# Pooled attention and a three-way maxout: the order of the first batch's loads, its size found in two steps, and a new order of the first seven groups

## The chip, the cores and the metric

The program runs on one core of one Trainium2 chip. The metric is the device time of one execution in microseconds (us): 1984.18 before, the median of three runs (1984.15 to 1985.3). The core has five engines with instruction queues of their own: TensorE (PE in the profile) multiplies matrices, VectorE (DVE), ScalarE (ACT) and GpSimd (POOL) work elementwise, and SyncE (SP) issues the DMAs here. Each engine takes its instructions in the order in which they are written; between engines and DMAs semaphores say what has to be done first.

## The reference

```python
kv_pool = kv.reshape(B, H // r, r, W // r, r, C).mean(axis=(2, 4))   # B=4, H=384, W=32, r=4, C=128
k = v = kv_pool.reshape(B, -1, C) @ w_sr                             # 768 keys in each batch
s = (q @ k.transpose(0, 2, 1)) / np.sqrt(C)                          # q: 4 x 12288 x 128
a = np.exp(s - s.max(-1, keepdims=True))
a /= a.sum(-1, keepdims=True) + 1e-09
x = (a @ v).reshape(-1, C)                                           # 49152 x 128
h = np.maximum(np.maximum(x @ w1, x @ w2), x @ w3)                   # 768 hidden columns
out = h @ w_out
```

The four weights of the last two lines come as float64. The kernel takes them apart with integer operations on their two 32-bit words.

## The kernel before

The 49152 rows of q are cut into 96 groups of 512 rows, 24 for each batch, and a group into 4 tiles of 128 rows. Nearly every product is made in three float16 matmuls: each operand is split into a high part and the remainder (`_hi` and `_lo`, or `hh`/`hl`, `xh`/`xl`), and the product of the two remainders is left out. The split needs a power of two for a scale, so each operand's largest value is found first.

The program is one list of steps, written out as tokens in the strings of START, STEADY and END (lines 159 to 214). `run` (line 1026) reads them in order, and `step` (line 888) takes the next piece of work of that kind. START covers the loads, the weights and the first groups; STEADY, two groups long, is run 45 times; END finishes the last groups. The place of a token sets the place of its instructions on each engine. Their meaning:

- `S`: one tile's 128 x 768 scores on PE, 6 matmuls, into `ps_s`, which has two buffers. `m`: the row maximum `mx` and the bias `nb` on DVE. `e`: the exponential `a` on ACT, which frees `ps_s`. `c`: its float16 part on ACT, into `ahl`, which has three buffers. `l`: the remainder on POOL, and then the DMA that turns the tile into `aT`.
- `X`: half of a group's attention product on PE (18 matmuls of 512 columns); for group 0 a quarter, one tile at a time (`attend_tile`). `xh`, `xl`: its split on ACT and DVE.
- `H`: one of six hidden steps of a group, 6 matmuls into the two buffers of `ps_h`. `R`: the first of its two halves on ACT. `M`: the maximum `h` of both on DVE. `C`, `L`: its split, on ACT and POOL. `O`: the output product, 3 matmuls (6 with the last hidden step of a group). The third of the three hidden products is avoided: two are made with differences of the weights (`d_hi`, `d_lo`), and `w1` comes in through one product `w1o` of w1 and w_out.
- `P`, `G`, `T`: the output is turned by a DMA (`o_turned`), merged and scaled on DVE, and stored.
- `qd`, `qc`, `qp`, `qe`, `qh`, `ql`: load of q, its scaling by column on POOL, its size, and its split and turn.
- `kd`, `ka`: load and pooling of the next batch's kv. In START the first batch has tokens of its own: `kv.s.i` loads piece i of third s (512 KB each, 12 pieces), `add` and `fold` sum pieces on DVE (or POOL), `gat` and `end` sum 128 columns at a time on PE by matmuls with the identity, `gathered_peak` takes the third's maximum, `turn_tops` and `tops` the maximum over thirds and partitions (by one matmul and a reduction), `sized` the scale `k_up` from it, `gathered_project` multiplies by w_sr, and `gathered_hi`, `gathered_lo` write the keys `k_hi`, `k_lo`.
- `w` and a letter, with the weight and its half: `wd` loads, `wm` scales the upper words (ACT), `ws`, `wl`, `wn` put the words together on DVE (`w_e`), `wr` takes the difference from w1 (POOL), `wt` the maximum, `dsize`, `dsized` the scale, `wh`, `wo` the split.

A `!` behind a token puts it on DVE, a `%` on POOL (for `qp!`, the sum on ACT). The kv pieces and the weight halves share the 13 buffers of `kvp`, which are given out in turn, so the fourteenth load waits until the first one's readers are done, and so on. SP's queue is in order too: a load that waits for its buffer holds up all that is issued behind it, turns (DMA_TRANSPOSE) included. At the end, `last_hidden` and `last_max` (lines 734 and 748) do the last hidden step in two halves, and `last_project` and `last_finish` the last output.

Of the kernel before, what the change touches and what calls it, by code (L numbers as in the profile page):

```python
# [20 lines left out]
def kernel(  # L21
# [338 lines left out]

    def turn_w1(h):
# [705 lines left out]
```

## Time and profile before

| | us |
|---|---|
| median of three runs | 1984.18 |
| the profiled execution | 1984.26 |
| its span, first to last instruction | 1982.5 |
| PE busy in the span | 1957.7 |
| ACT busy | 1491.2 |
| DVE busy | 1451.0 |
| POOL busy | 1314.9 |

The granted TensorE clock is 1.00 over the span. PE is the engine to watch: what it is idle, or what its work grows by, is the time that a change can move. All instructions carry one line, L104, that of the helper which keeps the written order, so the rows are read by the names of tiles: output, arrow, inputs, then partitions x elements and type, and the count. Times in the rows are us from the span's start.

### The profile page before, as it was taken

Reading aid. Unit: us, or ns where it says so; the run is one execution under the profiler, and the core shown is the slowest. Engines: PE = TensorE matmul, PEld = TensorE weight load, DVE = VectorE, ACT = ScalarE, POOL = GpSimd, SP = SyncE. Lnnn points to the kernel's source line nnn. Section 1 sums busy time; section 2 is a strip of 40 time slices with the busy share of each in tenths; the row PEclk is TensorE's granted clock in tenths of the full one; section 3 lists DMA queues with packets and bytes.
Section 4 is the critical chain, followed back from the end, with each engine's and each line's share of the span. In section 5 each row is a group of like instructions: output and inputs, shape, how many; then the busy total and the mean of one; then the engine's idle time right before and its main releaser. Section 6 shows DMA issues by size and latency. Waiting matters only on the chain.

```text
span 1982.5 us, 29471 instructions
## 1 busy us (share of the span) xinstructions
PE 1957.7 (99%) x9813; PEld 959.1 (48%) x9813; DVE 1451.0 (73%) x2531; ACT 1491.2 (75%) x2617; POOL 1314.9 (66%) x959
## 2 busy tenths in 40 slices
PE   5999999999999999999999999999999999999999
PEld 5544444444444444444444444444444444444444
DVE  8777777777766777777767777777767666767677
ACT  4777777777777777777777777777777777777774
POOL 3577766766666666766766666766676666666653
PEclk9999999999999999999999999999999999999999
DMA  8677776676678777766668667866677666756663
GB/s 276 122 150 161 169 153 137 129 143 135 127 154 163 156 154 152 141 139 136 132 126 168 153 147 165 162 125 133 136 137 142 126 125 125 150 121 126 132 128 81
DMA packets 844761, 284.50 MB, mean 144 GB/s; under 512 B 818240, under 2 KB 819392, under 8 KB 844608
## 3 DMA queue, kind: packets, MB, share of 16 engines
q1 hardware_dynamic: 844608, 282.61, 69.6%
q8 instruction: 77, 1.26, 0.3%
q14 instruction: 76, 0.62, 0.1%
HBM read 53.54 MB, written 25.17 MB: 40 GB/s over the span
## 4 chain that ended last, share of the span: by engine, by line
PE 96%; DMA 2%; DVE 1%; ACT 0%; POOL 0%; issue 0%; SPq 0%; DVEq 0%; ACTq 0%
PE ps_h L104 37%; PE ps_o L104 22%; PE ps_x L104 19%; PE ps_s L104 18%; DMA aT<-ahl 1%; DMA kv_piece<-in_kv_dram 1%; DMA kv_piece<-in_moe_w_dram 0%; POOL ahl L104 0%; DMA o_turned<-o_planes 0%; DVE kv_piece L104 0%; DVE w_e L104 0%; SPq L104 0%; ACT a L104 0%; DVE mx L104 0%; DVE o_sb L104 0%
## 5 line engine op out<-in xcount | busy, mean ns | idle before, releaser
L104 POOL TENSOR_TENSOR hl<-h,hh 128x512 f16<-128x512 f32 x473 | 566.3, 1203 | 488.4 <-ACT hh L104 487.4
L104 POOL TENSOR_TENSOR ahl<-a,ahl 128x768 f16<-128x768 f32 x382 | 635.3, 1682 | 119.6 <-ACT ahl L104 79.8
L104 DVE SCALAR_TENSOR_TENSOR h<-ps_h,h 128x512 f32<-128x512 f32 x575 | 396.7, 690 | 372.9 <-PE ps_h L104 214.3
L104 ACT ACTIVATE h<-ps_h 128x512 f32<-128x512 f32 x575 | 342.6, 596 | 282.6 <-PE ps_h L104 272.4
L104 PE MATMUL ps_h<-xh,d_hi 128*128 128x512 f16 x1150 | 435.8, 379 | 0.3 <-DVE h L104 0.2
L104 PE MATMUL ps_h<-xl,d_hi 128*128 128x512 f16 x1150 | 435.8, 379 | 0.0
L104 PE MATMUL ps_h<-xh,d_lo 128*128 128x512 f16 x1150 | 435.8, 379 | 0.0
L104 DVE TENSOR_REDUCE mx<-ps_s 128x1 f32<-128x768 f32 x384 | 365.5, 952 | 55.2 <-PE ps_s L104 55.0
L104 ACT ACTIVATE a<-ps_s,nb,q_sc 128x768 f32<-128x768 f32 x384 | 379.1, 987 | 6.3 <-DVE nb L104 5.1
L104 PE MATMUL ps_s<-k_hi,qT 128*128 128x384 f16 x1536 | 374.8, 326 | 4.9 <-ACT a L104 4.5
L104 PE MATMUL ps_x<-aT,v_hi 128*128 128x512 f16 (+1 forms) x1188 | 366.6, 373 | 0.7 <-DMA aT<-ahl 0.6
L104 ACT CAST hh<-h 128x512 f16<-128x512 f32 x577 | 335.3, 613 | 42.0 <-DVE h L104 41.4
L104 PEld LDWEIGHTS <-d_hi 128*128 128x128 f16 x2308 | 225.7, 98 | 256.5 <-issue 0.3
L104 PE MATMUL ps_o<-hh,wo 128*128 128x512 f16 x1140 | 339.0, 379 | 0.0
L104 PEld LDWEIGHTS <-qT 128*128 128x128 f16 x2304 | 225.3, 98 | 194.0 <-issue 6.8
L104 ACT CAST ahl<-a 128x768 f16<-128x768 f32 x375 | 306.4, 829 | 7.7 <-DMA aT<-ahl 1.9
L104 PEld LDWEIGHTS <-wo 128*128 128x128 f16 x1710 | 167.3, 98 | 191.8 <-DVE wo L104 0.2
L104 PE MATMUL ps_s<-k_lo,qT 128*128 128x384 f16 x768 | 250.4, 326 | 0.3 <-DVE k_lo L104 0.3
L104 PE MATMUL ps_x<-aT,v_lo 128*128 128x512 f16 (+1 forms) x594 | 220.2, 373 | 0.0
L104 PE MATMUL ps_o<-hl,wo 128*128 128x512 f16 x570 | 216.0, 379 | 0.0
L104 PEld LDWEIGHTS <-v_hi 128*128 128x128 f16 x1188 | 115.4, 98 | 135.0 <-DMA aT<-ahl 0.8
L104 PEld LDWEIGHTS <-d_lo 128*128 128x128 f16 x1154 | 112.9, 98 | 122.1 <-issue 2.5
(142 smaller groups left out, 1420.2 us busy)
## 6 DMA issues: line engine op xcount, KB each, us to landing
q_sb<-in_q_dram SPq DMA_DIRECT2D x48, 512.0 KB, 4.3
kv_piece<-in_kv_dram SPq DMA_DIRECT2D x48, 512.0 KB, 4.3
out_dram<-o_sb SPq DMA_DIRECT2D x95, 256.0 KB, 2.0
aT<-ahl SPq DMA_TRANSPOSE x384, 4.0
kv_piece<-in_moe_w_dram SPq DMA_DIRECT2D x6, 384.0 KB, 6.2
qT<-q_hl SPq DMA_TRANSPOSE x96, 3.6
o_turned<-o_planes SPq DMA_TRANSPOSE x95, 3.4
kv_piece<-in_moe_w_out_dram SPq DMA_DIRECT2D x2, 384.0 KB, 5.0
```

Of the source, the lines that this page charges most:

```text
L104: return lambda **kw: tc.keep_in_program_order(op(**kw))
```

## The change

It has five parts.

1. A new START. It covers seven groups where the old one covered one, and STEADY is run 42 times instead of 45; both give the same steps in all, and the steps done when the first common STEADY begins are the same. In its first strings q, one weight half (`wd.0.0`) and all twelve kv pieces are loaded, and the other weight halves behind them. The three `fold` steps are gone, and five `add`s (one of them on POOL, `add.0.0.1%`) stand where three stood, so that the gathers on PE go from 62 to 56.
2. The first batch's size is found in two steps. `early_tops` takes the maximum of thirds 0 and 2, over partitions too; `last_tops` brings that of third 1 alone; `first_sized` takes the larger one and makes the scale with integer operations (the exponent's bits and their complement) in place of a reciprocal; `first_exps` makes what hangs on it, later. The scale is another power of two than before, and g_exp and o_down follow it.
3. Tokens are taken apart: `lt`, `qt`, `Pt` and `Tt` issue the turns and the store that stood inside `l`, `ql`, `P` and `T`; `qu` is the second half of `qp`; `turned_w1` and `produced` the second halves of `turn_w1` and `product`. STEADY and END have the new tokens right behind the old ones.
4. The first tile's scores have the four matmuls with `k_hi` ahead of the two with `k_lo`; `gathered_project` for third 2 takes a buffer of `ps_s` instead of `ps_o`.
5. In END `last_max` stands ahead of the last but one group's `G` and `T`.

The core of the diff (of START, whose effect the rows further down show, only its first strings):

```diff
-    W_SIGNS = 3
+    W_SIGNS = 2
...
-        "sr qd qc! qc! srh wd.1.1 wm.1.1 wd.2.0 wm.2.0! ws.2.0 wd.0.0 ws.1.1 wl.2.0 wn.2.0 kv.2.1",
+        "qd wd.0.0 kv.2.2 kv.2.0 sr kv.2.1 kv.0.0 gat.2.2.4 kv.2.3 kv.0.1 wm.0.0! kv.0.3 qc! kv.0.2 qc! srh",
+        "kv.1.1 add.2.0.1 qp! kv.1.0 kv.1.2 gat.2.0.4 end.2.3.4 qu add.0.0.1% qh kv.1.3 ws.0.0 ql add.0.2.3",
...
-        "L! G T O last_hidden O O last_max last_project.3 last_project.4 last_project.5 last_finish",
+        "C L! L! O last_hidden O O last_max G T Tt last_project.3 last_project.4 last_project.5 last_finish",
...
-                self.kps[1] = ps_o.tile([P, NJ, C], F32, name="ps_o").rearrange("p j c -> p (j c)")
+                self.kps[1] = two_banks()[:, 0]
...
+        def early_tops(self, s, n):
+            dve.tensor_reduce(out=self.m[:, KS:KS + 1], in_=self.m[:, s:n + 1:n - s], axis=AX.X, op=ALU.max)
+            self.tops_ps = spare(True)
+            mm(out=self.tops_ps[:, :P], lhsT=self.m[:, KS:KS + 1].to_broadcast([P, P]), rhs=ident, start=True, stop=True)
+        def early(self):
+            self.least = tiny.tile([P, 1], F32, name="least", bufs=1)
+            dve.tensor_reduce(out=self.least, in_=self.tops_ps[:, :P], axis=AX.X, op=ALU.max)
+            dve.tensor_scalar(out=self.least, in0=self.least, scalar1=TINY, scalar2=None, op0=ALU.max)
+        def first_sized(self):
+            dve.tensor_scalar(
+                out=self.g, in0=self.g, scalar1=self.least, scalar2=2.0 ** -12, op0=ALU.max, op1=ALU.mult
+            )
+            dve.tensor_scalar(
+                out=self.up.bitcast(I32), in0=self.g.bitcast(I32), scalar1=EXPO, scalar2=EXPO,
+                op0=ALU.bitwise_and, op1=ALU.bitwise_xor,
+            )
...
+        terms = [(h, i) for h in range(2) for i in range(3)]
+        if (g, j) == (0, 0):
+            terms.sort(key=lambda t: t[1] == 2)
...
-    for _ in range(NG // 2 - 3):
+    for _ in range(NG // 2 - 6):
         run(STEADY)
```

On SP, at the start of the program, the loads stand as follows in before (-) and now (+). `in_moe_w_dram` are w1, w2 and w3, `in_kv_dram` the kv pieces.

```order
 L104 DMA wsr_sb<-in_w_sr_dram 128x128
 L104 DMA q_sb<-in_q_dram 128x1024
+L104 DMA kv_piece<-in_moe_w_dram 128x768
+L104 DMA kv_piece<-in_kv_dram 128x1x1024 x12
 L104 DMA kv_piece<-in_moe_w_dram 128x768 x3
-L104 DMA kv_piece<-in_kv_dram 128x1x1024
+L104 DMA q_sb<-in_q_dram 128x1024
 L104 DMA kv_piece<-in_moe_w_dram 128x768
-L104 DMA kv_piece<-in_kv_dram 128x1x1024 x4
+L104 DMA_TRANSPOSE qT<-q_hl 128x8x128
 L104 DMA kv_piece<-in_moe_w_dram 128x768
```

All twelve kv pieces have moved ahead of five of the six halves of w1, w2 and w3 and of the second load of q.

On DVE, from the first batch's keys on, these rows stood in before:

```order
L104 SCALAR_TENSOR_TENSOR k_lo<-ps_x,k_up,k_hi 128x512
L104 SCALAR_TENSOR_TENSOR k_lo<-ps_o,k_up,k_hi 128x256
L104 TENSOR_SCALAR w_e<-w_e 128x384
L104 TENSOR_REDUCE mx<-ps_s 128x1
L104 TENSOR_SCALAR nb<-mx,q_sc 128x1
L104 TENSOR_REDUCE mx<-ps_s 128x1
L104 TENSOR_SCALAR nb<-mx,q_sc 128x1
L104 TENSOR_SCALAR w_e<-w_e 128x384
L104 SCALAR_TENSOR_TENSOR w_e<-kv_piece,w_e 128x384 x3
```

And in the changed kernel, at the same place:

```order
L104 SCALAR_TENSOR_TENSOR k_lo<-ps_x,k_up,k_hi 128x512
L104 SCALAR_TENSOR_TENSOR k_lo<-ps_s,k_up,k_hi 128x256
L104 TENSOR_SCALAR w_e<-w_e 128x384
L104 SCALAR_TENSOR_TENSOR w_e<-kv_piece,w_e 128x384
L104 TENSOR_SCALAR q_sc<-q_row,g_exp 128x1
L104 TENSOR_REDUCE mx<-ps_s 128x1
L104 TENSOR_SCALAR nb<-mx,q_sc 128x1
L104 SCALAR_TENSOR_TENSOR w_e<-kv_piece,w_e 128x384
L104 TENSOR_REDUCE mx<-ps_s 128x1
L104 TENSOR_SCALAR nb<-mx,q_sc 128x1
L104 SCALAR_TENSOR_TENSOR w_e<-kv_piece,w_e 128x384
```

The weight passes (`w_e`) that before were mostly done by then stand between the row maxima now.

On DVE, at the end of the program, behind the last remainders of full width (`o_turned` is the last but one group's output, the 256 wide rows are the last hidden step's halves):

```order
-L104 COPY o_sb<-o_turned 128x2x512
-L104 TENSOR_SCALAR rs<-sm,o_down 128x4
-L104 RECIPROCAL rs<-rs 128x4
-L104 SCALAR_TENSOR_TENSOR o_sb<-o_sb,w_down,rs 128x512
-L104 SCALAR_TENSOR_TENSOR h<-ps_s,h_23182 128x256
-L104 SCALAR_TENSOR_TENSOR h<-ps_s,h_23186 128x256
+L104 SCALAR_TENSOR_TENSOR h<-ps_s,h_23172 128x256
+L104 SCALAR_TENSOR_TENSOR h<-ps_s,h_23176 128x256
 L104 TENSOR_TENSOR hl<-h,hh 128x256 x2
+L104 COPY o_sb<-o_turned 128x2x512
+L104 TENSOR_SCALAR rs<-sm,o_down 128x4
+L104 RECIPROCAL rs<-rs 128x4
```

The last hidden step's maxima and remainders have moved ahead of the merge and the scaling of the group before.

More of the change, by code (lines that the diff above doesn't have):

```diff
@@ L359, in sized_u, with keep_warm @@
         times(w1o_up, d_up[0], u_up[0], H_DOWN)
+    def keep_warm(n):
+        if "warm" not in st:
+            st["warm"] = ps_o.tile([P, G], F32, name="ps_o")
+        w = ident.bitcast(F16)
+        for _ in range(n):
+            mm(out=st["warm"][:, :2 * P], lhsT=w[:, :P], rhs=w, start=True, stop=True)
     def turn_w1(h):
@@ L365, in turn_w1, with turned_w1 @@
             tr(out=ps[:, t * P:(t + 1) * P], in_=W[0, h].values()[:, t * P:(t + 1) * P], identity=ident)
-        act.copy(out=w1T[h], in_=ps[:, :HALF_F])
+        W["turned", h] = ps
+    def turned_w1(h):
+        act.copy(out=w1T[h], in_=W.pop(("turned", h))[:, :HALF_F])
     def product_w1():
@@ L376, in product_w1, with produced_w1 @@
             )
+        W["product"] = ps
+    def produced_w1():
+        ps = W.pop("product")
         act.mul(out=w1o[:, 0], in_=ps[:, :C], mul=w1o_up)
@@ L452, in gathered_project, with gathered_hi @@
             )
-        def gathered_hi(self, n):
+        def gathered_hi(self, n, on=None):
             ps, ks = (self.kps[n], slice(0, G)) if n == 0 else (self.kps[n][:, :PW], slice(G, NK))
-            act.mul(out=self.k_hi[:, ks], in_=ps, mul=self.up)
+            if on:
+                on.tensor_scalar(out=self.k_hi[:, ks], in0=ps, scalar1=self.up, scalar2=None, op0=ALU.mult)
+            else:
+                act.mul(out=self.k_hi[:, ks], in_=ps, mul=self.up)
         def gathered_lo(self, n):
@@ L490, in peak, with turn_tops @@
             )
-        def turn_tops(self, first=False):
+        def turn_tops(self):
             dve.tensor_reduce(out=self.m[:, KS:KS + 1], in_=self.m[:, :KS], axis=AX.X, op=ALU.max)
-            self.tops_ps = spare(first)
+            self.tops_ps = spare(False)
             mm(
@@ L498, in turn_tops, with last_tops, first_exps @@
             )
+        def early_tops(self, s, n):
+            dve.tensor_reduce(out=self.m[:, KS:KS + 1], in_=self.m[:, s:n + 1:n - s], axis=AX.X, op=ALU.max)
+            self.tops_ps = spare(True)
+            mm(
+                out=self.tops_ps[:, :P], lhsT=self.m[:, KS:KS + 1].to_broadcast([P, P]), rhs=ident,
+                start=True, stop=True,
+            )
[3 more added lines that the diff above has]
+            dve.tensor_scalar(out=self.least, in0=self.least, scalar1=TINY, scalar2=None, op0=ALU.max)
+        def last_tops(self, s):
+            self.tops_ps = spare(True)
+            mm(
+                out=self.tops_ps[:, :P], lhsT=self.m[:, s:s + 1].to_broadcast([P, P]), rhs=ident,
+                start=True, stop=True,
+            )
+        def first_sized(self):
+            dve.tensor_scalar(
+                out=self.g, in0=self.g, scalar1=self.least, scalar2=2.0 ** -12, op0=ALU.max, op1=ALU.mult
+            )
+            dve.tensor_scalar(
+                out=self.up.bitcast(I32), in0=self.g.bitcast(I32), scalar1=EXPO, scalar2=EXPO,
+                op0=ALU.bitwise_and, op1=ALU.bitwise_xor,
+            )
+        def first_exps(self):
+            dve.tensor_scalar(
+                out=self.g.bitcast(I32), in0=self.g.bitcast(I32), scalar1=EXPO, scalar2=None, op0=ALU.bitwise_and
+            )
+            times(self.g_exp, self.g, SCALE * 2.0 ** -19)
+            times(self.o_down[:, 0:1], self.up, O_DOWN / A_UP)
+            times(self.o_down[:, 1:2], self.up, O_DOWN * 1e-9)
         def tops(self):
@@ L537 @@
     KT = {}
-    st = {x: {} for x in ("q", "qr", "ps", "qT", "sc", "sm", "nb", "aT", "x", "hp", "h", "a", "turned", "split", "qhl", "xh", "h1")}
+    st = {x: {} for x in ("q", "qr", "ps", "qT", "sc", "sm", "nb", "aT", "x", "hp", "h", "a", "turned", "split", "qhl", "xh", "h1", "ahl")}
     def q_load(s):
@@ L562, in q_peak, with q_up @@
             dve.tensor_reduce(out=row, in_=st["q"][s], axis=AX.XY, op=ALU.max, apply_absolute_value=True)
+        st["qr"][s] = row
+    def q_up(s):
+        row = st["qr"][s]
         up = qp.tile([P, 1], F32, name="q_up", bufs=2)
@@ L610, in scores @@
         st["ps"][g, j] = two_banks()[:, :, :HALF]
-        for h in range(2):
-            for i, (s_, kk) in enumerate(((0, k.k_hi), (1, k.k_hi), (0, k.k_lo))):
-                mm(
-                    out=st["ps"][g, j][:, h], lhsT=qT[:, j, s_], rhs=kk[:, h * HALF:(h + 1) * HALF],
-                    start=i == 0, stop=i == 2,
-                )
+        terms = [(h, i) for h in range(2) for i in range(3)]
+        if (g, j) == (0, 0):
+            terms.sort(key=lambda t: t[1] == 2)
+        for h, i in terms:
+            s_, kk = ((0, k.k_hi), (1, k.k_hi), (0, k.k_lo))[i]
+            mm(
+                out=st["ps"][g, j][:, h], lhsT=qT[:, j, s_], rhs=kk[:, h * HALF:(h + 1) * HALF],
+                start=i == 0, stop=i == 2,
+            )
     def soft_bias(g, j, negated):
@@ L645, in soft_lo, with soft_turn @@
         a, ahl = st["a"].pop((g, j))
+        (on or pool).tensor_tensor(out=ahl[:, 1], in0=a, in1=ahl[:, 0], op=ALU.subtract)
+        st["ahl"][g, j] = ahl
+    def soft_turn(g, j):
         if g not in st["aT"]:
             st["aT"][g] = ap_.tile([P, 2 * NKT, G], F16, name="aT")
-        (on or pool).tensor_tensor(out=ahl[:, 1], in0=a, in1=ahl[:, 0], op=ALU.subtract)
+        sp_dma.dma_start_transpose(
+            out=st["aT"][g][:, :, j * P:(j + 1) * P], in_=st["ahl"].pop((g, j)).rearrange("p s k -> p (s k)")
+        )
         st["split"][g] = st["split"].get(g, 0) + 1
-        sp_dma.dma_start_transpose(
-            out=st["aT"][g][:, :, j * P:(j + 1) * P], in_=ahl.rearrange("p s k -> p (s k)")
-        )
     def attend(g, part):
@@ L813, in turn_out, with turned_out @@
         copy_on(OUT_ON[0])(out=planes, in_=st.pop("oT").bitcast(U16).rearrange("c (t w) -> c w t", w=2))
+        st["turned"][g] = planes
+    def turned_out(g):
+        planes = st["turned"].pop(g)
         turned = op.tile([P, 2, NJ, C], U16, name="o_turned", bufs=2)
@@ L843, in scale_out @@
         )
-        store(g, 0, o)
+        st["turned"][g] = o
     def store(g, j, o):
@@ L903, in step @@
             soft_lo(*n, on)
+        elif token == "lt":
+            soft_turn(*n)
         elif token == "X":
@@ L933, in step @@
             q_peak(n, bool(on))
+        elif token == "qu":
+            q_up(n)
         elif token == "qe":
@@ L939, in step @@
             q_lo(n)
+        elif token == "qt":
+            q_turn(n)
+        elif token == "Pt":
+            turned_out(n)
+        elif token == "Tt":
+            store(n, 0, st["turned"].pop(n))
         elif token == "kd":
@@ L978, in start @@
             k.gather(s, i, width, False, True, us=u or range(KU))
-        elif name in ("gathered", "gathered_peak", "gathered_project", "gathered_hi", "gathered_lo", "value"):
+        elif name == "gathered_hi":
+            k.gathered_hi(*n, on)
+        elif name in ("gathered", "gathered_peak", "gathered_project", "gathered_lo", "value", "early_tops", "last_tops"):
             getattr(k, name)(*n)
-        elif name == "turn_tops":
-            k.turn_tops(True)
-        elif name in ("tops", "sized"):
+        elif name == "warm":
+            keep_warm(*n)
+        elif name in ("early", "tops", "first_sized", "first_exps"):
             getattr(k, name)()
@@ L997 @@
         "dsize": size_d, "dsized": sized_d, "ratio": ratio_u, "usize": size_u, "usized": sized_u,
[L998 removed]
+        "turn_w1": turn_w1, "turned_w1": turned_w1, "product": product_w1, "produced": produced_w1, "last_hidden": last_hidden, "last_max": last_max,
         "last_project": lambda f: last_project(NG - 1, f),
```

13 lines of the change are left out of this document (6 added, 7 removed), and 82 rows, old and new, of tables (END, START, STEADY).

## The prediction, made before the changed kernel ran

> **What bounds the kernel now.** I read the page first, then TensorE's busy time by stretches, then the chain of waits and the order of time of the first 100 us.
>
> ```profile
> span 1982.5 us, 29471 instructions
> PE 1957.7 (99%) x9813; PEld 959.1 (48%) x9813; DVE 1451.0 (73%) x2531; ACT 1491.2 (75%) x2617; POOL 1314.9 (66%) x959
> 0.00:10.00 10.00, 1.38 (x4) 1.00 (x4) 6.39 (x18) 2.35 (x4) 0.70 (x6) 1.00 0.79 284
> 10.00:20.00 10.00, 5.37 (x31) 5.40 (x32) 9.44 (x20) 3.93 (x7) 2.18 (x2) 1.00 1.03 410
> 20.00:30.00 10.00, 9.49 (x84) 9.21 (x82) 7.50 (x18) 2.53 (x6) 5.19 (x5) 1.00 1.04 329
> 30.00:40.00 10.00, 6.82 (x42) 5.01 (x43) 8.60 (x30) 6.16 (x12) 2.49 (x2) 1.00 0.63 178
> 40.00:50.00 10.00, 7.01 (x61) 4.73 (x59) 9.38 (x22) 8.18 (x15) 7.14 (x5) 1.00 0.81 173
> 50.00:60.00 10.00, 9.42 (x90) 6.72 (x88) 7.63 (x20) 7.37 (x15) 3.93 (x3) 1.00 0.63 111
> 60.00:70.00 10.00, 9.78 (x46) 4.22 (x45) 6.96 (x12) 7.43 (x15) 6.60 (x6) 1.00 0.61 115
> 1970.00:1982.50 12.50, 8.53 (x105) 6.57 (x103) 7.37 (x15) 3.87 (x8) 1.26 (x2) 0.95 0.40 65
> ```
>
> TensorE (PE) is idle for 1982.5 - 1957.7 = 24.8 us. The stretches say where: 8.62, 4.63, 0.51, 3.18, 2.99, 0.58 and 0.22 us in the first seven tens, 20.7 together, and 3.97 in the last stretch. In between it is busy throughout. So only the first 70 us and the tail can give anything, and at most about 25 us.
>
> ```profile
> 18.12 10.79 DMA kv_piece<-in_kv_dram
> 29.00 1.24 DVE kv_piece L104
> 30.29 2.07 PE ps_h L104 x16
> 32.38 0.44 DVE pool_max L104
> 34.60 0.70 ACT k_hi L104
> 38.27 1.07 ACT a L104 x2
> 40.47 0.73 ACT ahl L104
> 41.26 3.57 POOL ahl L104 x2
> 49.13 4.55 DMA aT<-ahl
> 53.72 1.17 PE ps_x L104 x18
> 54.88 0.97 PE ps_s L104 x6
> 58.30 1.29 PE ps_h L104 x6
> 65.18 0.65 PE ps_o L104 x3
> 67.77 3.88 PE ps_x L104 x18
> 93.37 1.29 PE ps_h L104 x6
> ```
>
> This is the chain: the last key piece lands at 28.91, its last gather ends at 32.36, the keys are scaled at 34.60 (k_hi). The softmax of the first four tiles follows; the last turned tile (aT) lands at 53.68, and then PE runs without real gaps. The rows also give PE's unit prices: 0.97 for a score tile (S), 1.29 for a hidden step (H), 0.65 for an output step (O), 1.94 for half an attention product (X), 1.17 for each of the four short ones of group 0.
>
> I call **lag** the time on the clock minus the PE work of these units done since the first score. The lag at the end is what a change in the start can move. At 94.66 before has done 17 S (16.5), 4 short and 4 half X (4.7 + 7.8), 13 H (16.8), 7 O (4.5) and 2.6 of work on w1 and sizes: 52.9. Its lag is 41.8, and PE has no gap after that.
>
> **The keys come earlier.** The order on SP now has q, one weight half and then all twelve kv pieces, where six halves and a second q stood among them. In front of the last piece lie 0.07 + 0.52 + 0.39 + 12 x 0.524 = 7.27 MB. The stretches show 284, 410 and 329 GB/s, so 6.94 MB by 20 us; the rest at 410 is there at 20.8, and I allow 1 us to landing: 21.8 instead of 28.9. VectorE (DVE) is then still at other work, to 22.2 by my sum of its list; the add takes 1.24 (23.45), the gather 2.07 (25.55), the maximum 0.44 behind weight passes (26.4). From that maximum to k_hi before takes 1.8 (32.82 to 34.60); I take 1.6, as the reciprocal and one pass over the size fall away, and the part of the first two thirds is ready before: k_hi at **28.0**, 6.6 us earlier. Bounds: 27.3 if DVE has no queue, 29.5 if the three weight passes ahead of the maximum wait for their halves. For SP now stops at the second weight half, which takes the buffer of the first: that is free only when DVE has finished the first half: the eighth kv piece is there at 16.7, its add ends at 17.9, two weight passes at 19. Behind it wait four more weight loads, q and the first qT turn; 1.8 us of kv are still in flight then, which covers the issue. Each us by which DVE is later there shifts them all.
>
> [...]
>
> **From there DVE is the bound.** These rows price its list.
>
> ```profile
> 35.98 0.48 DVE L104 SCALAR_TENSOR_TENSOR k_lo<-ps_o,k_up,k_hi 128x256 f16<-128x256 f32 x1
> 39.47 1.49 DVE L104 SCALAR_TENSOR_TENSOR w_e<-kv_piece,w_e 128x384 int32<-128x384 int32 x3
> 47.42 0.95 DVE L104 TENSOR_REDUCE mx<-ps_s 128x1 f32<-128x768 f32 x1
> 48.53 0.95 DVE L104 TENSOR_REDUCE mx<-ps_s 128x1 f32<-128x768 f32 x1
> 55.55 0.69 DVE L104 SCALAR_TENSOR_TENSOR xl<-ps_x,xh 128x512 f16<-128x512 f32 x1 [1.42 <-ACT xh L104]
> 55.70 0.38 PE L104 MATMUL ps_h<-xh,d_hi 128*128 128x512 f16 x1
> 57.43 0.69 DVE L104 SCALAR_TENSOR_TENSOR h<-ps_h,h 128x512 f32<-128x512 f32 x1
> L104 DVE TENSOR_REDUCE d_top<-w_e 128x1 f32<-128x384 f32 x6 | 3.1, 542 | 0.0
> L104 DVE SCALAR_TENSOR_TENSOR d_lo<-w_e,d_up,d_hi 128x384 f16<-128x384 f32 x4 | 2.8, 732 | 0.0
> L104 DVE SCALAR_TENSOR_TENSOR q_hl<-q_sb,q_up,q_hl x96: 733/744/1639, 25.1 to 1919.3; 128x512 f16<-128x512 f32 x96
> ```
>
> Start to start, a row maximum with its bias takes 1.11 (47.42 to 48.53), a weight pass 0.50, a hidden maximum (h) 0.61 or 0.62 (57.43 to the next start). For the rest I take the shortest means less the 0.05 by which neighbours overlap; d_lo 0.57, q_hl 0.70, a weight maximum 0.49, a one-column instruction 0.18. After the new k_hi come one weight pass, four small ones and the two k_lo (0.75 and 0.48, less the overlap): k_lo ends at 30.4, against 36.46 before. By the fifth hidden maximum the list then holds 11 maxima with bias (12.2), 11 weight passes and 4 short ones of 0.32 (6.8), 7 size maxima of weights of 0.49 (3.4), 4 d_lo (2.3), 2 q_hl (1.4), xl (0.65), 5 hidden maxima (3.1) and some 25 small ones (4.7): **34.6**, so 65.0 if DVE never waits. The first xl falls at 49.7, and the first H begins there instead of at 55.70.
>
> PE's work up to the half of the sixth H that needs this fifth maximum is 12 S (11.6), 4 short and 2 half X (8.6), 5.5 H (7.1) and 1.5 on w1 and sizes: 28.8. The lag from DVE's list is 36.2. I made the same sum for each hidden step. It stays at 34 to 36 up to the fifteenth (97 us) and falls from there, since from then PE has more to do than DVE. The same sum for before gives 38.1 at its first hidden maximum, and what came was 41.8: **3.7 above the list**. Of these, 1.4 are the wait of xl in the row at 55.55, for the aT that landed at 53.68. In the new order the fourth tile's cast on ACT (0.73, behind three exponentials of 1.07 and their casts) ends at about 41.3; POOL's subtraction (half of 3.57, at its best 1.65) ends at 43.0, aT lands 4.55 later, at 47.5, the last short X takes 1.17 and xh is done at 49.4: 0.3 before DVE asks for it, so that wait is just covered. Against this, DVE is the bound for 35 us longer, with every small wait on PE, ScalarE (ACT) or GpSimd (POOL) paid in full. I take 3.3 above the list: a lag of 39.5, **2.3 us less** than now. The bounds of this slip are 0.8 and, as a rival below, 11.
>
> PE's own work loses six gathers and gains one matmul; both lie ahead of the first score, where PE waits for the pieces anyway: nothing. The separate tokens that issue a turn or a store later on SP (lt, qt, Pt, Tt) change no work; they move the wait of SP behind other issues. STEADY and END have the same order on PE, and their loops begin with the same steps done: nothing.
>
> **The tail.**
>
> ```profile
> 1974.97 0.38 ACT L104 ACTIVATE h<-ps_s 128x256 f32<-128x256 f32 x1 [0.27 <-PE ps_s L104]
> 1975.33 0.74 DVE L104 COPY o_sb<-o_turned 128x1024 uint16<-128x1024 uint16 x1 [0.89 <-DMA o_turned<-o_planes]
> 1977.15 0.75 DVE L104 SCALAR_TENSOR_TENSOR h<-ps_s,h 128x256 f32<-128x256 f32 x2
> 1978.04 0.81 DVE L104 TENSOR_TENSOR hl<-h,hh 128x256 f16<-128x256 f32 x2
> 1979.25 0.47 DVE L104 SCALAR_TENSOR_TENSOR o_sb<-ps_x,w_down,rs 128x256 f32<-128x256 f32 x1
> ```
>
> Now DVE merges and scales the last but one group (1975.33 to 1977.15) before the last hidden maxima, and PE waits for them. With these ahead they can start at about 1974.75, behind ACT's first half; the second half waits for ACT until 1975.4, both remainders are done at 1976.6, before PE has finished what stands ahead, and the 1.8 us of scaling follow. The final scaling then ends at about 1979.3 instead of 1979.72. The three stores are issued closer together, so I count **0.3 us**, between 0 and 0.4.
>
> Sum against the profiled run's own 1984.26 us (span 1982.5 and 1.76 around it): 1984.26 - 2.3 - 0.3 = 1981.7. The median of the runs, 1984.18, is 0.08 away; I keep 1981.7.
>
> **Rivals.**
> 1. DVE keeps to its list, with a slip of under 1.5. For: k_hi, aT and xh meet DVE's asking times within some tenths, and the groups in the trace are mostly at their shortest durations. Against: the same sum missed before's lag by 3.7. Slip 1.1: 1979.5.
> 2. The load on DVE costs more than the early keys bring: slower. The first seven groups now put 10 casts, 7 exponential and 7 hidden remainders and 3 q products more on DVE (counted against START and three STEADY of before, which do the same steps), while POOL still runs.
>
> ```profile
> 56.87 1.65 POOL L104 TENSOR_TENSOR ahl<-a,ahl 128x768 f16<-128x768 f32 x1 [5.57 <-ACT ahl L104]
> 58.04 0.89 DVE L104 CAST ahl<-a 128x768 f16<-128x768 f32 x1
> L104 DVE CAST ahl<-a x9: 546/560/1039, 46.8 to 1942.2; 128x768 f16<-128x768 f32 x9
> L104 DVE SCALAR_TENSOR_TENSOR q_hl<-q_sb,q_up,q_hl x96: 733/744/1639, 25.1 to 1919.3; 128x512 f16<-128x512 f32 x96
> ```
>
> The cast at 58.04 met POOL's subtraction and took 0.89, not the 0.55 of the shortest: 0.34 lost. Up to the fifteenth hidden step 32 instructions on DVE are of the kinds that read two tiles or cast. If each pays that, 10.9 us stand in place of my 3.3: 1989.3. The gain is gone at a slip of 5.9, and the kernel is over 0.2% slower from 9.8; only what falls while DVE is the bound counts. Against it: the median of 96 q_hl is 744 ns, with 733 the least, so most meet nothing.
> [...]
> 3. The keys do not come as early as the order says, because SP's stop at the second half starves DVE of weights: k_hi at 31 or later, and the rest unchanged. The lag is then 42 or more and the tail alone is left: 1984.0.
>
> **How the numbers follow.** Forecast (slip 1.7 to 6.5; 1980.2 to 1985) 0.60, rival 1 0.22, rival 2 0.09, rival 3 0.09. 0.2% is 4.0 us, about what a measurement of this kernel can tell from no change. Faster by more than that needs a slip below 1.6: rival 1, 0.22. Slower by more needs 1988.2: rival 2 and a little over, 0.10. The rest, 0.68, is within. The range goes from a slip of 0.8 with a tail of 0.4 (1979.0) to a slip of 8.4 (1986.8), and leaves out most of rival 2 and little at the lower end.
>
> **What would show it.** Right: the last kv piece lands near 22, k_hi starts near 28, the first H near 50; DVE is over 95% busy from 30 to 95 us while PE has gaps of some tenths at hidden steps, waiting for DVE's h; the idle sum of PE in the first 110 us falls by about 2. Wrong: k_hi after 29.5; H waiting for ACT or for aT instead of DVE; DVE's casts and remainders with means far over 0.7 and 1.3; PE gaps after 110 us.

## The result, and the profile after

| | before | after |
|---|---|---|
| median of six runs, us | 1984.45 (1983.13 to 1985.37) | 1996.18 (1994.66 to 1998.05) |
| the profiled execution's span, us | 1982.5 | 1992.9 |
| PE busy, us | 1957.7 | 1964.0 |
| DVE busy, us | 1451.0 | 1482.8 |

The ratio is 1.0059, with a 95% interval of 1.0046 to 1.0072: the changed kernel is slower by 11.7 us. The forecast was 1981.7 us, no change that can be measured, with a range up to 1986.8. It was wrong. The profiled execution took 1994.66, the lowest of the six, 10.4 above the profiled one of before; the steps below are counted in that one.

The page of the changed kernel and PE's stretches of 10 us (columns as before: PE, PEld, DVE, ACT and POOL busy, then the granted clock, the DMA share and GB/s):

```profile
span 1992.9 us, 29467 instructions
PE 1964.0 (99%) x9803; PEld 959.6 (48%) x9803; DVE 1482.8 (74%) x2559; ACT 1481.2 (74%) x2605; POOL 1297.1 (65%) x943
...
20.00:30.00 10.00, 7.72 (x55) 6.05 (x54) 9.62 (x24) 3.91 (x8) 2.56 (x2) 1.00 1.12 335
30.00:40.00 10.00, 6.73 (x31) 3.59 (x30) 9.82 (x19) 7.36 (x13) 5.48 (x5) 0.83 0.96 223
40.00:50.00 10.00, 8.71 (x60) 5.52 (x59) 9.86 (x16) 6.56 (x13) 7.57 (x5) 0.66 0.65 124
50.00:60.00 10.00, 7.40 (x67) 4.78 (x68) 9.72 (x23) 8.73 (x17) 5.10 (x3) 1.00 0.97 166
60.00:70.00 10.00, 8.20 (x41) 3.73 (x39) 9.86 (x15) 6.02 (x11) 7.13 (x5) 1.00 0.24 67
70.00:80.00 10.00, 8.19 (x41) 3.91 (x40) 9.43 (x26) 6.97 (x13) 4.33 (x4) 1.00 0.37 70
```

DVE is busy 9.4 to 9.9 of every 10 us, as the forecast said. PE has gaps of 1.3 to 3.3 us in every stretch from 30 to 80, where before had hardly any from 50 on. Who PE waits for between 29 and 80 us (us in all, times, the longest):

```profile
PE ps_s L104 <- ACT a L104: 4.1, 4, 2.1
PE ps_h L104 <- DVE d_top L104: 3.0, 2, 2.6
PE ps_s L104 <- ACT w_e L104: 1.9, 1, 1.9
PE ps_h L104 <- DVE d_lo L104: 1.8, 1, 1.8
PE ps_h L104 <- DVE u_top L104: 1.7, 2, 1.4
```

Three of the five are DVE's weight work, 6.5 us. PE waits for none of the three behind 29 us in before, which has the size maxima `d_top` done at 32 us, while the changed kernel has five of them between 42 and 53 us. And DVE is late with this work. Its order of time around the first softmax tiles, with GpSimd's beneath:

```profile
35.53 1.57 DVE L104 TENSOR_SCALAR w_e<-w_e 128x384 int32<-128x384 int32 x1
37.02 0.94 DVE L104 TENSOR_REDUCE mx<-ps_s 128x1 f32<-128x768 f32 x1
64.12 1.96 DVE L104 SCALAR_TENSOR_TENSOR w_e<-kv_piece,w_e 128x384 int32<-128x384 int32 x1
74.13 0.69 DVE L104 SCALAR_TENSOR_TENSOR h<-ps_h,h 128x512 f32<-128x512 f32 x1
...
35.24 1.65 POOL L104 TENSOR_TENSOR ahl<-a,ahl 128x768 f16<-128x768 f32 x1 [0.58 <-ACT ahl L104]
37.09 1.64 POOL L104 TENSOR_TENSOR ahl<-a,ahl 128x768 f16<-128x768 f32 x1 [0.20 <-ACT ahl L104]
64.03 1.64 POOL L104 TENSOR_TENSOR ahl<-a,ahl 128x768 f16<-128x768 f32 x1
```

The weight pass at 35.53 takes 0.35 elsewhere. GpSimd began a subtraction at 35.24 and ended it at 36.89; the pass ended 0.21 later, at 37.10. The pass at 64.12 ended 0.41 after GpSimd's subtraction, at 66.08. The row maximum at 37.02, which reads PSUM, took its usual 0.94 beside a subtraction. The first `xl`, which the first hidden step waits for, started at 55.73, where the forecast had 49.7; the fifth hidden maximum started at 74.13, where it had 65.0, before any slip.

I call this lengthening **company**. To follow the loss I take the start of ACT's part of each hidden step, in every kernel, less the same step in before. In the middle of the new table the steps stand at other places among PE's other work, so single values there mean little; from step 49 on the orders agree and the difference no longer changes. For the changed kernel it is +0.2 at step 1, +9.2 at step 5, +7.4 at step 15 and **+10.8 from step 49 on**. Its keys came 6.8 us earlier, so that gain was already gone at the first hidden step.

### The profile page after: what moved, and what is told of

The parts are those of the page before. It is cut to its first block, busy times and chain, and to the rows that moved or that the text cites. A ratio compares the mean times of both kernels' runs of the same rounds, so it can differ in the third digit from the quotient of the medians.

```text
span 1992.9 us, 29467 instructions
## 1 busy us (share of the span) xinstructions
PE 1964.0 (99%) x9803; PEld 959.6 (48%) x9803; DVE 1482.8 (74%) x2559; ACT 1481.2 (74%) x2605; POOL 1297.1 (65%) x943
## 4 chain that ended last, share of the span: by engine, by line
PE 92%; DVE 5%; DMA 1%; issue 1%; ACT 0%; SPq 0%; POOL 0%; DVEq 0%; ACTq 0%; POOLq 0%
PE ps_h L104 36%; PE ps_o L104 21%; PE ps_x L104 18%; PE ps_s L104 18%; DVE mx L104 1%; DMA kv_piece<-in_kv_dram 1%; DVE w_e L104 1%; DVE h L104 1%; DVE ahl L104 0%; DVE hl L104 0%; DVE d_lo L104 0%; DVE kv_piece L104 0%; DMA q_sb<-in_q_dram 0%; SPq L104 0%; DVE q_hl L104 0%
## 5 line engine op out<-in xcount | busy, mean ns | idle before, releaser
L104 POOL TENSOR_TENSOR hl<-h,hh 128x512 f16<-128x512 f32 x466 | 560.2, 1208 | 499.3 <-ACT hh L104 497.0
L104 POOL TENSOR_TENSOR ahl<-a,ahl 128x768 f16<-128x768 f32 x375 | 624.5, 1684 | 137.8 <-ACT ahl L104 73.8
L104 ACT CAST ahl<-a 128x768 f16<-128x768 f32 x365 | 298.4, 828 | 6.1 <-DMA aT<-ahl 0.5
```

The lines of the kernel that those rows point to most:

```text
L104: return lambda **kw: tc.keep_in_program_order(op(**kw))
```

## The experiments

The theories: GpSimd's company on DVE (**T1**); PE's granted clock, which fell to 0.66 and 0.83 (**T2**); more work on DVE later on, by the casts and remainders that the new table puts there (**T3**); the order of the new table itself (**T4**).

**The end alone** (e1_end_order), on before:

```diff
-"L! G T O last_hidden O O last_max last_project.3 ...
+"L! O last_hidden O O last_max G T last_project.3 ...
```

> The kernel before with only the new order at the end: the merging and scaling of the last but one group behind the last hidden maxima. In the changed kernel's trace the last scaling comes 0.29 us earlier behind the same point of the last hidden step, but the end of the span only 0.10 us. Theory 'the end order gains 0.3 us, as predicted': 1984.1 against 1984.4. Theory 'it gains 0.1 us and the stores take the rest back': 1984.3. Theory 'a part of the 11.7 us comes from the end': 1986 or more. Timed runs hardly tell the first two apart; the trace's distance from the last hidden step's ACT instruction to the end of the span (8.18 us before) does.

1984.59, ratio 1.0000 (0.9990 to 1.0009). From the last hidden step's ACT row to the end of the span it is 8.13 us (1974.66 to 1982.8), against 8.14 before and 8.05 in the changed kernel. The last scaling ends 5.22 behind that row, 5.41 before. So the reorder wins some 0.2 us on DVE and the stores hand on less than 0.1.

**GpSimd quiet, its work on ACT** (e2_pool_quiet):

```diff
+        if 4 * g + j < 12 and not on:
+            act.copy(out=ahl[:, 1], in_=a)
...
-wr.1.0 wr.2.0 wr.1.1 wr.2.1
+wr.1.0! wr.2.0! wr.1.1! wr.2.1!
```

> The changed kernel with GpSimd kept quiet in the first 76 us: the remainders of the first twelve score tiles are replaced by a copy on ACT, so their low halves are wrong; the q column factors of groups 2 to 5 are left out (a copy on ACT in their place); the four weight differences w_e - w_e run on DVE (about 0.5 us each, 2 us more on DVE). Theory 'company': DVE's list was right and its instructions were lengthened by GpSimd's. Then the 13.7 us by which DVE's instructions between 26 and 76 us exceed their shortest durations fall below 3, the fifth hidden maximum comes near 64 to 66 us instead of 74.1, and the time is 1986 to 1989 (the loss of 3.6 us after 110 us stays). Theory 'granted clock': the time is lost on PE because its clock fell to 0.5 to 0.7 between 30 and 48 us; then the fifth maximum stays near 74 and the time at 1994 to 1998.

1995.19, ratio 1.0054 (1.0039 to 1.0069): no better. The lengthening was gone: summed over 26 to 76 us, DVE's durations exceed the shortest of their kind (same operation, tiles and shape, in any of the traces) by some 2 us instead of some 13. But DVE now waited 7.2 us for others, where the changed kernel had no such wait, and ACT was busy 9.97 of 10 us between 40 and 50. I had moved the bound, not tested it; e7 below repeats it without the load on ACT.

**The late casts on ACT** (e3_casts_act): `c!` becomes `c` sixteen times in START.

> The changed kernel with the 16 casts of exponentials that START's new table puts on DVE done on ACT instead (GpSimd's work unchanged). Theory 'load on DVE after 110 us': DVE was 93 to 96% busy there and PE waited for xl, h, hl and o_planes; 16 casts of 0.55 us and their 2.9 us of lengthening go, so most of the 3.6 us lost between hidden step 21 and step 49 come back: 1992 to 1994, with the fifth hidden maximum still at 74. Theory 'the order of the table itself makes those gaps': 1995 to 1998.

1997.03, ratio 1.0063 (1.0048 to 1.0078). DVE's idle time between 110 and 220 us rose from 11.0 to 15.5, and PE's gaps there stayed (3.6 us, now 3.2). The casts' load is not the cause.

**PE kept busy** (e4_warm):

```diff
-"kd qc S ...            "... wr.1.0 S qu ...         "... lt e S wt.1.0 ...
+"warm.14 kd qc S ...    "... wr.1.0 warm.6 S qu ...  "... lt e warm.8 S wt.1.0 ...
...
```

> The changed kernel with 39 idle matmuls (128x256) on PE in the gaps ahead of the first, third, fifth, sixth and seventh score tiles, so that PE is busy there. Theory 'granted clock': the clock stays at 1.00 between 30 and 48 us and the time falls by 4 to 6 us, to 1990 to 1992. Theory 'company': the clock may recover, but DVE sets the pace there, so the fifth hidden maximum stays at 73 to 75 us and the time at 1995 to 1997.

1996.14, ratio 1.0056 (1.0039 to 1.0072). The clock was 1.00 from 26 to 56 us, and step 1, at 57.5, stood at +0.8, no earlier than in the changed kernel (+0.2). Then the clock fell to half from 58 to 61 us, so step 5, at +10.3, tells less. But two of the four runs have a mean clock of 1.000, and they took 1994.32 and 1994.69: at full clock some 10 us are still lost. T2 is not the main cause.

**The old table in the new code** (e5_old_table): START and W_SIGNS of before, the split tokens behind their old places, and the size in two steps (shown against before):

```diff
-gathered_peak.2 gathered_peak.0 qd gathered.0 turn_tops ... tops ... sized gathered_hi.0
+gathered_peak.2 early_tops.1.2 gathered_peak.0 early last_tops.0 qd gathered.0 ... tops ... first_sized gathered_hi.0 first_exps
```

> The changed kernel's code with the START table of before (split tokens put right behind their old places, the last size of k found in two steps, the end in the new order); STEADY is the same in both. Theory 'the table of the first seven groups is the whole loss': 1983.5 to 1985, perhaps some tenths under before for the two-step size. Theory 'the new code (separate turns, split size, buffers) costs something': 1988 or more.

1985.67, ratio 1.0006 (0.9997 to 1.0016). All but 1.2 us of the loss is the table. The two steps gain nothing in the old order: k_hi starts at 35.82 instead of 34.60, since the early maximum's way over PE (0.98 of waiting) stands in front of the last one.

**The new table up to 78 us, then the old order** (e6_hybrid):

> The changed kernel with its START table up to the seventh hidden step (78 us), and from there the order of before's START and STEADY with what is already done taken out. The changed kernel has lost about 7 us by 100 us and 3.6 more between 110 and 220 us. Theory 'the late loss is made by the late part of the table': no PE gaps after 110 us, 1992 to 1993.5. Theory 'the late loss is handed on from the backlog of the first 80 us': 1995.5 to 1998.

1989.99, ratio 1.0030 (1.0020 to 1.0041). Step 5 is at +9.4 as in the changed kernel, but from step 13 on nothing is lost any more: +5.6 to the end. So the late part of the table costs 5.2 (10.8 - 5.6), more than the 3.6 that I had read off between steps.

**The early work of GpSimd left out, and its control** (e7_no_pool, e8_pool_apart). Both:

```diff
+        n = 1 if 4 * g + j < 12 else 2
+            out=st["aT"][g][:, :n * NKT, j * P:(j + 1) * P],
+            in_=st["ahl"].pop((g, j))[:, :n].rearrange("p s k -> p (s k)"),
...
-for i, (v, a) in enumerate(((k.v_hi, NKT + kt), ...
+for i, (v, a) in enumerate(((k.v_hi, (NKT if g >= 3 else 0) + kt), ...
```

e7_no_pool alone:

```diff
+        if 4 * g + j >= 12:
             (on or pool).tensor_tensor(out=ahl[:, 1], in0=a, in1=ahl[:, 0], op=ALU.subtract)
...
+        if g < 6 and not on:
+            return
         (on or pool).tensor_tensor(out=t, in0=t, in1=col_row...
...
-            (on or pool).tensor_tensor(out=self.e, in0=self.e, in1=W[0, self.h].e, op=ALU.subtract)
+            return
```

> The changed kernel with no work at all on GpSimd up to 76 us, and nothing put on another engine for it: left out are the remainders of the first twelve score tiles (only the high halves are transposed, and PE multiplies by these twice in place of the low ones), the column factors of q groups 2 to 5 and the four weight differences. The copies on ACT of the earlier run, which made ACT 92 to 100% busy, are gone. Theory 'company': with GpSimd quiet DVE keeps its listed durations and the fifth hidden maximum comes at 63 to 67 instead of 74; the time falls by 5 to 9 us against the next run. Theory 'another engine or the order bounds the stage at nearly the same level': DVE gets idle time, and the time falls by less than 2 us.

> The control of the run before it: the same halved transposes (only high halves, multiplied twice by PE) of the first twelve tiles, but GpSimd still does its remainders, column factors and weight differences; nobody waits for the remainders. The difference of the two is what GpSimd's company alone costs. Theory 'company': DVE's instructions between 26 and 76 us still exceed their shortest by 10 us or more, the fifth hidden maximum stays at 71 to 75 us, and the time 1994 to 1997. Theory 'the low halves are what PE waited for': the time falls to about the one of the run before.

With GpSimd at work 1994.88, ratio 1.0055 (1.0040 to 1.0070); without, 1984.95, ratio 1.0001 (0.9992 to 1.0011). At step 49 they stand at +10.8 and +0.8. In the control neither PE nor ACT nor DVE waits for GpSimd between 26 and 76 us, so what e7_no_pool takes away is its company alone (GpSimd is busy 28.1 us there in the control, and 7.0 us in e7_no_pool, by later work that has moved up). **GpSimd's company before 76 us costs 10.0 us**, and the missing low halves cost or gain nothing: the control is the changed kernel again, step for step. In e7_no_pool the fifth hidden maximum starts at 64.17, where the forecast's list had 65.0. DVE's groups of 26 to 76 us in the changed kernel, then in e7_no_pool (ns: shortest, median, longest, then the first and last start):

```profile
L104 DVE SCALAR_TENSOR_TENSOR w_e<-kv_piece,w_e x12: 545/924/1998, 27.6 to 69.2; 128x384 int32<-128x384 int32 x12
L104 DVE TENSOR_SCALAR w_e<-w_e x5: 350/351/1569, 26.5 to 60.2; 128x384 int32<-128x384 int32 x5
L104 DVE SCALAR_TENSOR_TENSOR d_lo<-w_e,d_up,d_hi x4: 609/1278/1986, 52.9 to 66.0; 128x384 f16<-128x384 f32 x4
L104 DVE SCALAR_TENSOR_TENSOR q_hl<-q_sb,q_up,q_hl x2: 736/1435/2134, 46.5 to 72.2; 128x512 f16<-128x512 f32 x2
L104 DVE TENSOR_REDUCE d_top<-w_e x5: 540/543/545, 42.6 to 52.4; 128x1 f32<-128x384 f32 x5
L104 DVE TENSOR_REDUCE mx<-ps_s x11: 941/945/950, 31.9 to 63.0; 128x1 f32<-128x768 f32 x11
```

```profile
L104 DVE SCALAR_TENSOR_TENSOR w_e<-kv_piece,w_e x13: 546/550/1407, 25.6 to 60.1; 128x384 int32<-128x384 int32 x13
L104 DVE TENSOR_SCALAR w_e<-w_e x5: 340/350/360, 26.9 to 53.8; 128x384 int32<-128x384 int32 x5
L104 DVE SCALAR_TENSOR_TENSOR d_lo<-w_e,d_up,d_hi x4: 607/609/614, 48.1 to 59.0; 128x384 f16<-128x384 f32 x4
L104 DVE TENSOR_REDUCE mx<-ps_s x14: 939/948/959, 31.6 to 72.8; 128x1 f32<-128x768 f32 x14
```

Two kinds of instruction stretch here: those that read two SBUF tiles (w_e from two, up to 2.00 us for 0.55; d_lo, up to 1.99 for 0.61; q_hl, up to 2.13 for 0.74), and the short pass over one tile (w_e from w_e, up to 1.57 for 0.35). The reductions do not, from SBUF (d_top, 540 to 545 ns) or PSUM (mx, 941 to 950), nor do the hidden maxima, which read one of their two operands from PSUM (0.67 to 0.69 each).

**Both cures** (e9_hybrid_no_pool: the edits of e6 and e7 together):

> Both cures together: no work on GpSimd up to 76 us as in e7_no_pool (the same work left out), and before's order from the seventh hidden step on as in e6_hybrid. Theory 'two separate losses that add': 10.0 us from GpSimd's company and 5.2 us from the late table, against a gain of about 4.4 from the earlier keys: 1979 to 1981, 4 to 5 us under before. Theory 'one backlog, seen twice': no better than the better of the two alone, 1984 to 1986.

1979.12, ratio 0.9974 (0.9964 to 0.9984); -4.8 from step 13 on. The two losses add. What is left out here is work that the output needs, so this is no kernel to keep; it shows about what the earlier keys would be worth.

**Remainders back to GpSimd** (e10_late_flags): `l!` becomes `l` and `L!` becomes `L` behind the fourteenth string of START.

> The changed kernel with the 8 exponential and 17 hidden remainders that the new START table puts on DVE after the seventh hidden step given back to GpSimd (the casts stay on DVE, the order stays). DVE sheds 8 x 0.95 + 17 x 0.68 = 19 us between 90 and 220 us, GpSimd gets some 33 us. Theory 'DVE is overloaded there': the late loss of 3.6 to 5.2 us goes, 1991 to 1993. Theory 'the order of the steps on PE makes the gaps': 1995 to 1998. GpSimd's longer work may also bring more company, or remainders that come late for PE: 1998 or more.

1997.87, ratio 1.0066 (1.0051 to 1.0081). DVE's idle time between 110 and 220 us rose from 11.0 to 20.0 us, PE's gaps there grew from 3.6 to 5.3, and the time did not fall. T3 falls for the second time: DVE with less of its own work and more company is no faster.

**Less GpSimd, nothing left out** (e11_hybrid_less_pool): e6_hybrid with `wr.x.y!` four times and `qc!` four times.

> e6_hybrid with the four weight differences and the column factors of q groups 2 to 5 on DVE, so that GpSimd runs 8 instructions (some 10 us) less before 76 us; nothing is left out. DVE gets 4 x 0.51 + 4 x 0.68 = 4.8 us more. Theory 'company costs about what the same work costs on DVE' (11 us over some 20 instructions of GpSimd, 0.56 each, so 8 x 0.56 = 4.5 saved): 1989 to 1991, as e6_hybrid (1990). Theory 'these eight carry most of the company': 1985 to 1988.

1990.60, ratio 1.0029 (1.0018 to 1.0040), as e6_hybrid (its profiled run, 1992.65, was the highest of its seven, so its steps are not compared). An instruction moved from GpSimd to DVE costs there about what its company cost.

**Company for before** (e12_before_company):

```diff
+    def busy_pool():
+        t = tiny.tile([P, NK], F32, name="scratch", bufs=1)
+        nc.vector.memset(t, 0.0)
+        for _ in range(12):
+            pool.tensor_tensor(out=t, in0=t, in1=t, op=ALU.subtract)
```

> The kernel before with 12 subtractions on a scratch tile (128x768) added on GpSimd at the start, where it is idle and DVE does its weight passes (about 3 to 28 us); nobody reads the scratch tile. Theory 'company': DVE's excess over shortest durations in the first 26 us rises from 2.1 us by 0.5 to 1.0 for each of the 12, to 8 to 14 us; DVE is 94% busy between 10 and 20 us, so k_hi comes later by most of it and the time is 1988 to 1996. Theory 'the changed kernel's instructions are long for another reason (its buffers, its order)': 1984 to 1985.

1995.92, ratio 1.0057 (1.0042 to 1.0072). Twelve instructions for which nobody waits cost 11.3 us. GpSimd's and DVE's order of time:

```profile
1.89 19.56 POOL L104 TENSOR_TENSOR scratch<-scratch 128x768 f32<-128x768 f32 x12 [0.59 <-DVE scratch L998]
...
10.44 1.38 DVE L104 TENSOR_SCALAR col_ones<-ones,col 128x128 f32<-128x128 f32 x1
11.73 0.28 DVE L104 SCALAR_TENSOR_TENSOR wsr_hl<-wsr_sb,wsr_hl 128x128 f16<-128x128 f32 x1
11.94 1.62 DVE L104 TENSOR_SCALAR w_e<-kv_piece 128x384 f32<-128x384 f32 x1
13.59 3.05 DVE L104 TENSOR_SCALAR w_e<-w_e 128x384 int32<-128x384 int32 x2
16.56 3.56 DVE L104 SCALAR_TENSOR_TENSOR w_e<-kv_piece,w_e 128x384 int32<-128x384 int32 x2
```

GpSimd's take 1.63 each (19.56 / 12), and nearly every DVE instruction of the two kinds takes 1.4 to 1.8, for 0.29 to 0.55 alone. About one gets through for each of GpSimd's: six lengthened ones in the 9.7 us from 10.44 to 20.12, in which GpSimd does 5.9 of 1.63. DVE's excess in the first 26 us is some 13, against some 2. Some of the rest of the delay may be PE's clock, which was 0.57 in the mean between 20 and 30 us.

**GpSimd out of the first seven groups** (e13_no_pool_longer, shown against e7_no_pool):

```diff
-        if 4 * g + j >= 12:
+        if on or g > 6:
             (on or pool).tensor_tensor(out=ahl[:, 1], ...
...
+        if g < 7 and not on:
+            st["h"][g, f] = (hh, hh)
+            return
         hl = hp.tile([P, G], F16, name="hl", bufs=HB_)
```

> e7_no_pool with GpSimd kept out of the whole stretch of the new table (to some 230 us), and nothing put elsewhere: left out, beside what e7_no_pool leaves out, are the remainders that GpSimd makes of the exponentials and hidden tiles of the first seven groups (the high halves are multiplied again in their place) and the column factors of q up to group 15. DVE keeps all its own work and the order stays the changed kernel's. Theory 'company makes the late loss too': the gaps of PE after 110 us go, and the time falls from e7_no_pool's 1985 to 1979 to 1981, as with before's late order. Theory 'the order alone': DVE's instructions get short, but PE's gaps stay and so does the time, 1984 to 1986.

1979.80, ratio 0.9979 (0.9969 to 0.9988); -4.4 at step 49. The order is the changed kernel's, and the late loss of 5.2 is gone too. GpSimd still makes 17 remainders of later groups, from 159 us on. The stretch 110 to 220 us, first in the changed kernel, then here, then in e6_hybrid:

```profile
110.00:220.00 110.00, 106.43 (x517) 50.25 (x516) 99.03 (x148) 66.19 (x122) 57.43 (x38) 1.00 0.66 136
```

```profile
110.00:220.00 110.00, 108.89 (x533) 51.98 (x532) 96.94 (x160) 69.44 (x127) 25.29 (x17) 1.00 0.55 116
```

```profile
110.00:220.00 110.00, 110.00 (x543) 53.03 (x542) 83.54 (x140) 85.15 (x150) 77.70 (x55) 1.00 0.77 159
```

PE's idle time there falls from 3.57 to 1.11. This run has no control like e8's: the missing remainders also shorten the way to the transposes. But in the changed kernel neither PE nor ACT nor DVE waits for GpSimd or aT between 76 and 232 us. PE's waits, to 220 us:

```profile
PE ps_h L104 <- DVE xl L104: 1.0, 2, 0.6
PE ps_h L104 <- DVE h L104: 1.0, 3, 0.5
PE ps_o L104 <- DVE o_planes L104: 0.8, 1, 0.8
PE ps_o L104 <- DVE hl L104: 0.8, 2, 0.4
PE ps_h L104 <- ACT h L104: 0.2, 1, 0.2
```

And what stands ahead of them on DVE is lengthened; for o_planes, it is the first of these two rows, which takes 0.75 alone:

```profile
138.24 1.88 DVE L104 SCALAR_TENSOR_TENSOR o_sb<-o_sb,w_down,rs 128x512 f32<-128x512 f32 x1
140.03 1.21 DVE L104 COPY o_planes<-ps_o 128x1024 uint16<-128x1024 uint16 x1
```

Summed over 110 to 220 us, DVE's durations exceed the shortest of their kind by 15.0 us in the changed kernel, by 6.9 here and by 5.3 in e6_hybrid, although GpSimd is busiest there (77.7 us, against 57.4 in the changed kernel). So company most likely makes the late loss as well, and T4 says where it strikes: the order of before keeps DVE's instructions clear of it (PE without a gap there, e6), the new one does not. Without a control this part is argued and not shown.

## Why the prediction was wrong, point by point

- **The keys come earlier: right.** The last kv piece was added at 22.42 (forecast 22.2), k_hi started at 27.81 (28.0), k_lo ended at 30.54 (30.4). From 10 to 20 us 413 GB/s were moved, as the sum had taken from before's 410.
- **DVE's list: right, as a list.** 34.6 us from there, to 65.0 at the fifth hidden maximum; with GpSimd's early work left out it came at 64.17 and 63.21 (e7, e13).
- **The slip above the list: wrong, and this is the step that failed.** I took 3.3 us, from the 3.7 that before showed. It was 16.4: before's lag of 41.8 plus the 10.8 lost, less the list's 36.2. Of it 10.0 are company before 76 us (e7 against e8), and 5.2 went with GpSimd's later work (e13 against e7, without a control). Without both, 1.2 are left, near the 1.1 of rival 1, which gave 1979.5 where e13 has 1979.8; that is in part luck, as e13's fifth hidden maximum stood 1.8 ahead of the list. Before's 3.7 said nothing of the new order: in before 21 of the 27 weight passes `w_e` started at 7 to 26 us, where GpSimd was busy 5.0 of 19 us. In the new order 17 run at 26 to 76 us, beside the softmax, where GpSimd is busy 28.2 of 50 us.
- **Rival 2 had the mechanism and lost on its price and its chance.** The price of 0.34 came from a single meeting, the cast at 58.04. In the changed kernel, 26 to 76 us, the 23 instructions of these four groups (busy us, mean ns)

```profile
L104 DVE SCALAR_TENSOR_TENSOR w_e<-kv_piece,w_e 128x384 int32<-128x384 int32 x12 | 13.0, 1087 | 0.0
L104 DVE SCALAR_TENSOR_TENSOR d_lo<-w_e,d_up,d_hi 128x384 f16<-128x384 f32 x4 | 5.1, 1288 | 0.0
L104 DVE TENSOR_SCALAR w_e<-w_e 128x384 int32<-128x384 int32 x5 | 3.6, 716 | 0.0
L104 DVE SCALAR_TENSOR_TENSOR q_hl<-q_sb,q_up,q_hl 128x512 f16<-128x512 f32 x2 | 2.9, 1435 | 0.0
```

  exceed their shortest by 6.5, 2.7, 1.8 and 1.4: 12.4 us in all, 0.54 each. GpSimd's share and half its mean instruction would give less (an estimate of 0.56 x 1.41 / 2 = 0.40, from 20 instructions in 28.2 us). The 32 instructions that I counted come to 17.3 us at 0.54; that this is close to 16.4 is in part chance, as the 16.4 holds also what was lost behind the fifteenth step, and as the count left out the short passes over one tile, which lost 1.8. The chance of 0.09 rested on the median of 96 q_hl: nearly all of those run in the steady loop, whose order keeps them clear of GpSimd (median 744 ns, the shortest 733), and say nothing of another order. Single rows lost several times the price of 0.34: 1.57 us for 0.35 and 1.96 for 0.55, beside GpSimd instructions of 1.64.
- **"From then PE has more to do than DVE" (behind the fifteenth step): right as a sum, wrong in what I took from it.** PE was busy 106.4 and DVE 99.0 of the 110 us behind 110, but DVE's instructions, lengthened by 15.0 us in all, still made PE wait there. The part of the loss that falls behind 76 us is 5.2 us (e6).
- **Rival 3, a DVE starved of weights: not met.** DVE never waited between 26 and 76 us.
- **PE's own work unchanged: not quite.** PE is busy 6.3 us more. Most of it is the clock, at 0.83 and 0.66 in two stretches of 10 us (an estimate of 5.1 us, by 0.17 and 0.34 of 10). As e4 shows no gain from a full clock there, this took the place of idle time.
- **The tail: a mis-sized term.** 0.3 us forecast; DVE's last scaling came 0.28 earlier, the end of the span about 0.1.

## What to carry to other kernels

The sum of durations on DVE held only for the company that its instructions kept: the fifth hidden maximum, at 65.0 by the sum, came at 64.17 without GpSimd's early work (e7) and at 74.13 with it. Before moving two-tile or short one-tile passes beside GpSimd's work, add a price for each. Here GpSimd's busy share times half its instruction was too low (0.40 against the 0.54 measured), and no row lost more than 1.45 us. But the order decided more than the share: in e6 GpSimd is busier behind 110 us (77.7 us, against 57.4), and DVE loses a third of what it loses in the changed kernel (5.3 us, against 15.0). An order that has been running well can hide such meetings, so its medians don't price a new order: the median of q_hl was 744 ns in before, and the two at 26 to 76 us in the changed kernel took 736 and 2134. A quick test of a suspected meeting is to give the old kernel the same company on a scratch tile (11.3 us lost in e12).

## What the runs showed of the hardware

In the changed kernel PE's granted clock fell to half after short pauses. Stretches of 2 us there:

```profile
28.00:30.00 2.00, 0.68 (x4) 0.41 (x5) 1.97 (x6) 1.29 (x3) 2.00 (x2) 1.00 1.02 323
30.00:32.00 2.00, 1.94 (x7) 0.80 (x6) 2.00 (x6) 1.59 (x3) 1.20 (x2) 0.56 1.10 397
32.00:34.00 2.00, 1.63 (x7) 0.95 (x5) 1.97 (x5) 0.78 (x1) 0.34 (x1) 0.59 1.22 154
```

PE had a pause of 1.94 us that ended at 29.32. The two stretches behind it are short of full clock by 0.44 and 0.41; at half clock that is 3.4 us ((0.44 + 0.41) x 2 / 0.5). Not each such pause did it: e7_no_pool had PE idle for some 2.7 us around 29 us (0.27, 2.00 and 0.45 us of its stretches of 2 us from 26 to 32), and kept 1.00.

What decides seems to be how a pause falls on a grid. In the changed kernel the clock is at 0.50 from 30.23 to 33.65 and from 40.47 to 47.30, and at 1.00 for 6.82 us between: one, two and two steps of 3.41 us. The low stretches of e3_casts_act add up to such steps too (6.8, 3.4 and 3.4 us, up to 80 us), and so do those of e4_warm (3.4 and 3.4). The pause in the changed kernel lies in one step, the first row here. In e7_no_pool the longer one is shared by two stretches of this length; as its clock is 1.00 from 20 to 240 us, no row shows where its own steps lie:

```profile
26.82:30.23 3.41, 1.41 (x9) 0.59 (x8) 3.18 (x11) 1.49 (x3) 2.79 (x3) 1.00 0.93 235
30.23:33.65 3.42, 3.40 (x11) 1.71 (x11) 3.38 (x8) 2.03 (x4) 0.97 (x2) 0.50 1.15 267
```

```profile
25.87:29.28 3.41, 1.86 (x11) 1.06 (x9) 3.06 (x14) 1.79 (x4) 0.00 (x0) 1.00 1.44 130
29.28:32.69 3.41, 2.23 (x15) 1.50 (x16) 2.76 (x7) 1.79 (x3) 0.00 (x0) 1.00 1.10 364
```

From 13.2 us to 80 us the changed kernel has two steps at full clock in which PE was busy 0.41 or less of the time (1.41 us from 26.82, 1.30 from 37.06), and half clock followed both. It followed none of its other steps at full clock, where PE was busy 0.47 or more (the least 1.62 us, from 64.36). In before, along steps of 3.41 us from 18.5 to 80 us, PE was busy 0.46 or more (the least 1.57 us, from 42.39), and the clock stayed at 1.00. Two cases are few for a rule.

Where it strikes seems to decide its price. In the profiled runs of the changed kernel and of e8 (1994.66 and 1994.67) the clock was low around 31 and 45 us, where PE waits for DVE anyway. In those of e3, e4 and e10 (1997.27 to 1997.67) it was low around 59 and 76 us, while hidden steps ran; there step 2 stands 1.5 to 2.0 us later than in the changed kernel, and step 49 at +13.3 to +13.8. That this makes the spread of the changed kernel's runs (3.4 us, against 2.2 before) fits, and so do the four runs of e4: the two with a mean clock of 1.000 took 1994.32 and 1994.69, the two with 0.998 took 1997.60 and 1997.67. It was not tested by itself.
